# Channel attention with an ELU feed-forward on one core: six row groups multiplied as split float32r parts, squares summed in PSUM

## The chip, the cores and the metric

One core of a Trainium2 chip runs the whole program in one launch. The metric is device time in microseconds (us), from a few runs of the same kernel on the same chip; lower is better. Inputs are float32, except that the two weight matrices are read as 64-bit numbers and converted on the chip.

## The reference, cut to what matters

```python
# q, k, v: (4, 6080, 256); w_in: (256, 2048); w_out: (2048, 256)
qn = q / (np.linalg.norm(q, axis=1, keepdims=True) + 1e-06)
kn = k / (np.linalg.norm(k, axis=1, keepdims=True) + 1e-06)
s = kn.transpose(0, 2, 1) @ qn / tau          # (4, 256, 256)
a = np.exp(s - s.max(-1, keepdims=True))
a /= a.sum(-1, keepdims=True) + 1e-09
x = (v @ a).reshape(24320, 256)
h = x @ w_in
out = np.where(h > 0, h, np.exp(np.minimum(h, 0)) - 1) @ w_out
```

For each of the four batches a 256 x 256 matrix of products of k and q (the gram) is summed over 6080 rows, scaled by the norms of the columns of q and k, and put through a softmax. The result is multiplied into w_in once per batch, so that the long part is v times a 256 x 2048 matrix, ELU, and a product with w_out.

## The kernel before, in words

**Engines.** TensorE (PE) multiplies. ScalarE (ACT) and VectorE (DVE) apply ELU and split numbers into a float32r part and a residue; three passes of float32r parts (high by high, high by low, low by high) then stand for one float32 product. Float32 operands can also be given to TensorE as they are; each such multiplication stands in the trace as two matmul records. GpSimd (POOL) and SyncE (SP) mostly issue DMAs.

**The head: batch 0's gram and norms.** The 6080 rows of q and k are cut into 23 full groups (two rows for each of 128 partitions, q and k together 0.5 MB) and a last "ragged" one. `load0` issues the loads from SP. For each group, `square_rows` (L183) squares q and k on ACT (L189, 128 x 1024 numbers) and adds the squares on DVE into `acc` (L190); three tiles of squares take turns. `gram0_item` multiplies the group five steps later in the program (`BEHIND = 5`): four float32 multiplications of 128 x 128 by 128 x 256 (`multiply`, L496), that is eight records, which add into two banks of PSUM. PE, DVE and ACT run in the order in which the code is written (a manual schedule). When the squares are summed, `norms0` folds the two halves of `acc` on DVE (L221), sums over the partitions with four narrow matmuls into `pn` (L224), takes the root on ACT (L203), works out the reciprocals on DVE and writes a diagonal matrix `dg` (L236). `spread` (L262) turns that into a row for every partition with a matmul. Then come the softmax (`softmax0`, L269 to L283), the transposes of its result (L290) and the products of w_in with it (L323). Between these steps PE gets `early_items`: single rows of batch 1's gram, which add into the PSUM tile `pe`.

**PSUM.** There are eight banks of 128 x 512 float32 numbers. Two belong to the tag "gram", three to "w", three to "o". In the kernel before, the three banks of "o" are three tiles: `pe` (the gram of batch 1; later the ring `gram_ring`: grams, norms, transposes and the products with w_in of the later batches) and `po_1` for two halves `dt` of the output (`po_of["o"]`, later used by every second chunk). The sums of squares stand in SBUF (`new_acc`).

**The rest of the program.** Four chunks of batch 0 are run in an order written out by hand (`take`). All else, from about 235 us on, is a list of operations with costs and due times, which a planner puts in an order for each engine (`plan_half`, `plan_rows`, `plan_soft`, `plan_s`, `best_plan`). The change does not touch the planner, its costs or its due times. In this part PE writes `po` (L1387 to L1389) and `pe` (rows of the next batch's gram at L1524, products with w_in at L1425 to L1427), and ACT reads finished sums out of them: the output copies (L1118, `o_both<-po`), the scaled products (L1430, `w<-pe,sums`), the roots of the norms (L1593), the transposed softmax (L1657).

**How waits are set.** The program is written with tiles. The framework looks, tile by tile, for accesses that must not be reordered (a read after a write, a write after a read), and sets semaphore waits between the engines: a reader of a tile waits for the write it depends on, and a later writer of the tile waits for that reader.

Of the kernel before, what the change touches and what calls it, by code (L numbers as in the profile page):

```python
# [9 lines left out]
F32 = mybir.dt.float32  # L10
F32R = mybir.dt.float32r
# [45 lines left out]
def channel_attention_then_elu_ffn(ctx: ExitStack, tc, q, k, vT, tau, w_in, w_out, outT):  # L57
# [8 lines left out]
    nc = tc.nc  # L66
    B, N, C = q.shape
# [112 lines left out]
            fill_left(raw, b)  # L180
        return raw

    def square_rows(raw, acc, first, sq=None):  # L183
        if first:
            nc.scalar.activation(acc, raw, AF.Square)
            return
        if sq is None:
            sq = work.tile([P, 2, 2, C], F32, tag="sq", bufs=1, name="sq")
        x = nc.scalar.activation(sq, raw, AF.Square)  # L189
        return x.ins, nc.vector.tensor_add(acc, acc, sq).ins  # L190

    def new_acc(b):
        return work.tile([P, 2, 2, C], F32, tag="acc", bufs=1, name=f"acc_{b}")
# [291 lines left out]
    half = {c: scratch(c, k=DT) for c in range(M)}  # L485
    sq1 = scratch(M - 1, k=2 * 2).rearrange("p (t r) c -> p t r c", t=2)

    acc = new_acc(0)
    pg0 = [ps.tile([P, 2, C], F32, tag="gram", bufs=KT, name=f"gram_0_{ct}") for ct in range(KT)]
    wi64, wo64, vraw, vts = {}, {}, {}, {}  # L490
    state = {}

    def multiply(raw, r, gram, first, last):

        for ct in range(KT):
            nc.tensor.matmul(  # L496
                gram[ct], raw[:, 1, r, ct * P : ct * P + P], raw[:, 0, r, :], start=first[ct], stop=last[ct]
            )
# [4 lines left out]
    with tc.manual_schedule(engines={nc.sync.engine}):  # L503
# [38 lines left out]
            load0(x)  # L542
        raw1 = [scratch(x, k=2 * 2).rearrange("p (t r) c -> p t r c", t=2) for x in range(M)]

        def gram0_item(x):
            raw = raws.pop(x)
            for r in range(2):
                multiply(raw, r, gram0, [x + r == 0] * KT, [x == FULL - 1 and r == 1] * KT)
            if x + DEEP < FULL:
                load0(x + DEEP)  # L550
            if x + DEEP == FULL - 1:
                wi64[0] = load_w_in(0)

        for x in range(FULL):
            if x >= BEHIND:
                gram0_item(x - BEHIND)
            summed = square_rows(raws[x], acc, x == 0, squares[x % 3])
            if x == 16:
                square_rows(ragged, acc, False, squares[0])
                for r in range(2):  # L560
                    multiply(ragged, r, gram0, none, none)
                itau = tiny.tile([P, 1], F32, name="itau")
                nc.vector.reciprocal(itau, tau_sb)
# [6 lines left out]
        def go_on(part, n):  # L570
            for _ in range(n):
                next(part, None)

        for x in range(FULL - BEHIND, FULL):
            if x == FULL - 2:
                go_on(parts[0], 1)
                pn, dg, rk, nm = norms0(acc, lambda: go_on(parts[0], 2))
                go_on(parts[0], 2)
                go_on(parts[1], 1)
            gram0_item(x)  # L580

        pe = ps.tile([P, KT, C], F32, tag="o", bufs=8 - KT - WB, name="pe")
        gram1 = [pe[:, ct, :] for ct in range(KT)]

        def early_items(n, count=[0]):
            for _ in range(n):
                x, r = divmod(count[0], 2)
                count[0] += 1
                multiply(raw1[x], r, gram1, [x == 0 and r == 0, False], [False, (x, r) == (EARLY - 1, 1)])

        spread(pn, dg)
        vraw[1] = load_v(1)
        raw1.append(work.tile([P, 2, 2, C], F32, tag="raw", bufs=5, name="raw_early"))
# [15 lines left out]
        at_once(parts[1])  # L609
        for kt in range(KT):  # L610
            split_v_lo(0, vraw[0], vts[0], kt)
        early_items(3)
        aT0 = transpose_a(a0)
        go_on(first_w_out, 1)
        early_items(3)
# [137 lines left out]
    def s_part(fq, x, name):  # L753
# [3 lines left out]
    steps = [(c, f) for c, lo, hi in pieces for f in range(lo, hi)]  # L757
    es, gs, pos = {}, {}, {}
    po_of = {
        "o": [ps.tile([P, CH], F32, tag="o", bufs=8 - KT - WB, name=f"po_1{dt}") for dt in range(DT)],  # L760
        "gram": [ps.tile([P, CH], F32, tag="gram", bufs=KT, name=f"po_0{dt}") for dt in range(DT)],
    }

# [973 lines left out]
```

## Time and profile before

| | us |
|---|---|
| median of three runs | 2063.54 (2063.24 to 2063.66) |
| the profiled execution's own time | 2063.12 |
| its span | 2061.3 |
| PE busy in the span | 2054.8 |
| POOL busy in the span | 60.7 |

The profile is of one execution. A row of its timeline gives the start in us from the span's start, the length in us, the engine, the line of the kernel, the operation, output<-input, the shapes, and how often it stands there; in brackets, how long the engine was idle before it and what ended the idle time. Matmuls overlap: a record is longer than the distance to the next one, and its end is modelled. The granted TensorE clock is 1.0 throughout.

### The profile page before, as it was taken

Reading aid. Unit: us, or ns where it says so; the run is one execution under the profiler, and the core shown is the slowest. Engines: PE = TensorE matmul, PEld = TensorE weight load, DVE = VectorE, ACT = ScalarE, POOL = GpSimd, SP = SyncE. Lnnn points to the kernel's source line nnn. Section 1 sums busy time; section 2 is a strip of 40 time slices with the busy share of each in tenths; the row PEclk is TensorE's granted clock in tenths of the full one; section 3 lists DMA queues with packets and bytes.
Section 4 is the critical chain, followed back from the end, with each engine's and each line's share of the span. In section 5 each row is a group of like instructions: output and inputs, shape, how many; then the busy total and the mean of one; then the engine's idle time right before and its main releaser. Section 6 shows DMA issues by size and latency. Waiting matters only on the chain.

```text
span 2061.3 us, 28054 instructions
## 1 busy us (share of the span) xinstructions
PE 2054.8 (100%) x9976; PEld 1812.9 (88%) x9976; DVE 1669.3 (81%) x2597; ACT 1721.0 (83%) x3120; POOL 60.7 (3%) x118
## 2 busy tenths in 40 slices
PE   9999999999999999999999999999999999999999
PEld 8888888899888888888988888888888888888888
DVE  7988989888889787887887878788789777677775
ACT  6888789897888888888888888888887788887886
POOL 0000000000100000000000000000001000000000
PEclk9999999999999999999999999999999999999999
DMA  9453232212332121121322212212124110110000
GB/s 360 130 151 102 102 108 72 86 49 96 101 109 68 61 87 57 62 71 44 114 93 93 78 36 89 66 62 77 42 100 135 41 57 16 41 56 16 21 30 21
DMA packets 71805, 164.94 MB, mean 80 GB/s; under 512 B 7536, under 2 KB 16752, under 8 KB 69616
## 3 DMA queue, kind: packets, MB, share of 16 engines
q1 hardware_dynamic: 55968, 118.53, 16.9%
q0 software_dynamic: 15408, 44.11, 6.8%
q8 instruction: 78, 1.28, 0.3%
q14 instruction: 63, 0.52, 0.1%
q10 hardware_dynamic: 288, 0.51, 0.1%
HBM read 100.40 MB, written 31.20 MB: 64 GB/s over the span
## 4 chain that ended last, share of the span: by engine, by line
PE 99%; ACT 0%; DVE 0%; DMA 0%; SPq 0%; issue 0%; ACTq 0%
PE bank_b L1329 16%; PE po L1387 15%; PE po L1388 14%; PE po L1389 14%; PE bank_e L1329 11%; PE bank_a L1329 11%; PE pe L1524 4%; PE gram L496 2%; PE po L422 1%; PE po L420 1%; PE po L421 1%; PE ph L380 1%; PE ph L381 1%; PE ph L382 1%; PE pe L1427 1%; PE pe L1426 1%
## 5 line engine op out<-in xcount | busy, mean ns | idle before, releaser
L1387 PE MATMUL po<-g,wo 128*128 128x512 f32 (+1 forms) x938 | 354.1, 377 | 0.0
L1388 PE MATMUL po<-g,wo 128*128 128x512 f32 (+1 forms) x938 | 353.4, 377 | 0.0
L1389 PE MATMUL po<-g,wo 128*128 128x512 f32 (+1 forms) x938 | 353.4, 377 | 0.0
L1360 ACT ACTIVATE more_e<-more_e 128x512 f32<-128x512 f32 (+1 forms) x563 | 344.6, 633 | 2.4
L1369 DVE TENSOR_TENSOR g<-more_e,g 128x512 fp32r<-128x512 f32 (+1 forms) x374 | 252.6, 681 | 54.7 <-ACT g L1366 50.1
L1366 ACT CAST g<-more_e 128x512 fp32r<-128x512 f32 (+1 forms) x374 | 228.6, 620 | 42.7 <-DVE more_e L1363 27.1
L1389 PEld LDWEIGHTS po<-g,wo 128*128 128x128 f32 x938 | 177.4, 189 | 22.8
L1387 PEld LDWEIGHTS po<-g,wo 128*128 128x128 f32 x938 | 177.5, 189 | 21.9 <-ACT o_both L1118 0.2
L1363 DVE SCALAR_TENSOR_TENSOR more_e<-more_e,bank_b 128x512 f32<-128x512 f32 (+1 forms) x141 | 96.0, 681 | 124.3 <-ACT more_e L1360 124.0
L1388 PEld LDWEIGHTS po<-g,wo 128*128 128x128 f32 x938 | 177.6, 189 | 21.2
L1357 ACT ACTIVATE more_e<-bank_b 128x512 f32<-128x512 f32 (+1 forms) x141 | 83.8, 595 | 126.5 <-PE bank_b L1329 125.8
L1387 PE MATMUL po<-wp,wo 128*128 128x512 f32 (+1 forms) x470 | 177.4, 378 | 0.1
L1388 PE MATMUL po<-wp,wo 128*128 128x512 f32 (+1 forms) x470 | 177.1, 377 | 0.0
L1389 PE MATMUL po<-wp,wo 128*128 128x512 f32 (+1 forms) x470 | 177.1, 377 | 0.0
L1369 DVE TENSOR_TENSOR wp<-more_e,wp 128x512 fp32r<-128x512 f32 (+1 forms) x189 | 128.6, 681 | 33.1 <-ACT wp L1366 31.8
L1329 PE MATMUL bank_e<-term,wp 128*128 128x512 f32 (+1 forms) x528 | 141.4, 377 | 0.0
L1366 ACT CAST wp<-more_e 128x512 fp32r<-128x512 f32 (+1 forms) x189 | 116.9, 620 | 21.1 <-DVE more_e L1363 17.8
L1338 DVE TENSOR_TENSOR bank_e<-bank_b,e 128x512 f32<-128x512 f32 (+1 forms) x176 | 121.1, 688 | 7.5 <-ACT e L1336 4.9
L1342 DVE TENSOR_TENSOR e<-bank_b,e 128x512 f32<-128x512 f32 (+1 forms) x176 | 119.6, 680 | 4.9 <-PE bank_b L1329 4.5
L1329 PE MATMUL bank_a<-term,wp 128*128 128x512 f32 (+1 forms) x456 | 122.0, 376 | 0.0
L1524 PEld LDWEIGHTS pe<-rows 128*128 128x128 f32 x804 | 110.4, 191 | 6.7
L1524 PE MATMUL pe<-rows 128*128 128x256 f32 x804 | 111.2, 275 | 0.0
(323 smaller groups left out, 4718.2 us busy)
## 6 DMA issues: line engine op xcount, KB each, us to landing
v<-in_v_dram SPq DMA_DIRECT2D x13, 1024.0 KB, 5.0
out_dram<-o_both SPq DMA_DIRECT2D x48, 256.0 KB, 2.0
wi<-wi_scr POOLq DMA_DIRECT2D x12, 1024.0 KB, 5.5
w<-in_q_dram SPq DMA_DIRECT2D x34, 256.0 KB, 2.7
w<-in_k_dram SPq DMA_DIRECT2D x34, 256.0 KB, 2.9
v<-in_v_dram SPq DMA_DIRECT2D x8, 992.0 KB, 4.8
more<-in_q_dram SPq DMA_DIRECT2D x30, 256.0 KB, 2.6
more<-in_k_dram SPq DMA_DIRECT2D x30, 256.0 KB, 2.9
```

Of the source, the lines that this page charges most:

```text
L1329: nc.tensor.matmul(into, ws[x], y, start=(begin and k == 0), stop=(k == 2), skip_group_check=True)
L1338: up = op(DVE, 0.605 * share, t + DUE["up"], lambda: nc.vector.tensor_add(ve, vb, p7.slot[:, 0:n]), [m6, keep], uses=[bank_b, bank_e, p7])
L1342: last = op(DVE, 0.605 * share, t + DUE["last"], lambda: nc.vector.tensor_add(vp(), vb, vp()), [m5, up], uses=[bank_b, p7])
L1357: nc.scalar.activation(ev(), h(), AF.Relu, scale=-1.0)
L1360: nc.scalar.activation(ev(), ev(), AF.Exp, scale=-1.0)
L1363: nc.vector.scalar_tensor_tensor(ev(), ev(), -1.0, h(), op0=ALU.add, op1=ALU.max)
L1366: nc.scalar.copy(g_part(g, 0, n), halves(ev()))
L1369: nc.vector.tensor_sub(g_part(g, 1, n), halves(ev()), g_part(g, 0, n).bitcast(F32))
L1387: nc.tensor.matmul(o, wo[:, f, 0, ds], hi, start=begin, stop=False)
L1388: nc.tensor.matmul(o, wo[:, f, 1, ds], hi, start=False, stop=False)
L1389: nc.tensor.matmul(o, wo[:, f, 0, ds], lo, start=False, stop=end)
L1524: nc.tensor.matmul(pg, r.tile[:, kx, 1, z, cs], in_turns(r.tile[:, qx, 0, z, :]), start=(g == begun and ct == 0 and z == 0 and m == 0), st ...
```

## The change

Three things are changed.

1. Six of the 23 groups (7, 10, 13, 16, 18 and 20) are split into a float32r part and a residue. The residues are made by GpSimd (`tensor_sub`); the float32r parts by GpSimd for groups 7, 16, 18 and 20, and by ACT for 10 and 13. The parts lie in a tile of the tag "vt", of which there are two. Such a group is multiplied in twelve float32r passes (`multiply_split`) instead of four float32 multiplications.
2. The sums of batch 0's squares stand in PSUM: in the first two of the three banks of tag "o". The last addition writes its sum to a tile in SBUF.
3. The three banks of "o" are made one tile, `out_banks`, for the whole program; the two `po_1` and `pe` are now slices of it.

Besides, the norms are taken one group later (before group 22 instead of group 21), and one of the early items is moved from behind the spread to ahead of it.

```diff
@@ square_rows @@
-    def square_rows(raw, acc, first, sq=None):
+    def square_rows(raw, acc, first, sq=None, to=None):
...
-        return x.ins, nc.vector.tensor_add(acc, acc, sq).ins
+        return x.ins, nc.vector.tensor_add(acc if to is None else to, acc, sq).ins
@@
-    acc = new_acc(0)
+    out_banks = ps.tile([P, (8 - KT - WB) * CH], F32, tag="o", bufs=1, name="out_banks")
+    acc = out_banks[:, 0 : 2 * CH].rearrange("p (t r c) -> p t r c", t=2, r=2)
...
+    def split_rows(raw, own):
+        parts = work.tile([P, 2, 2, 2, C], F32R, tag="vt", bufs=2, name="parts")
+        (nc.gpsimd.tensor_copy if own else nc.scalar.copy)(parts[:, 0], raw)
+        nc.gpsimd.tensor_sub(parts[:, 1], raw, parts[:, 0].bitcast(F32))
+        return parts
+
+    def multiply_split(parts, r, gram, last):
+        for ct in range(KT):
+            for m, (kx, qx) in enumerate(((0, 0), (0, 1), (1, 0))):
+                nc.tensor.matmul(
+                    gram[ct], parts[:, kx, 1, r, ct * P : ct * P + P], parts[:, qx, 0, r, :], start=False, stop=last and m == 2
+                )
@@ the loop over the groups @@
+        SPLIT0 = {7: True, 10: False, 13: False, 16: True, 18: True, 20: True}
+        split0 = {}
...
-                multiply(raw, r, gram0, [x + r == 0] * KT, [x == FULL - 1 and r == 1] * KT)
+                if x in split0:
+                    multiply_split(split0[x], r, gram0, x == FULL - 1 and r == 1)
+                else:
+                    multiply(raw, r, gram0, [x + r == 0] * KT, [x == FULL - 1 and r == 1] * KT)
...
-            summed = square_rows(raws[x], acc, x == 0, squares[x % 3])
+            if x == FULL - 1:
+                squared = new_acc(0)
+            square_rows(raws[x], acc, x == 0, squares[x % 3], squared if x == FULL - 1 else None)
+            if x in SPLIT0:
+                split0[x] = split_rows(raws[x], SPLIT0[x])
...
-            if x == FULL - 2:
+            if x == FULL - 1:
                 go_on(parts[0], 1)
-                pn, dg, rk, nm = norms0(acc, lambda: go_on(parts[0], 2))
+                pn, dg, rk, nm = norms0(squared, lambda: go_on(parts[0], 2))
...
-        pe = ps.tile([P, KT, C], F32, tag="o", bufs=8 - KT - WB, name="pe")
+        pe = out_banks[:, 2 * CH : 3 * CH].rearrange("p (k c) -> p k c", k=KT)
...
+        early_items(1)
         spread(pn, dg)
...
-        early_items(3)
+        early_items(2)
         aT0 = transpose_a(a0)
@@
-        "o": [ps.tile([P, CH], F32, tag="o", bufs=8 - KT - WB, name=f"po_1{dt}") for dt in range(DT)],
+        "o": [out_banks[:, dt * CH : (dt + 1) * CH] for dt in range(DT)],
```

Three places show what this does to the built program. The first is ACT in the head, at groups 10 to 14 (`raw_10`, `raw_11`, `raw_12`, then two in `room`; `sq`, `scr` and `sq_107` are the three tiles of squares); after the change, lines behind the new functions have numbers 16 to 27 higher. Before:

```order
L189 ACTIVATE scr<-raw_10_140 128x1024
L189 ACTIVATE sq_107<-raw_11_143 128x1024
L189 ACTIVATE sq<-raw_12_146 128x1024
L189 ACTIVATE scr<-room_87 128x1024
L189 ACTIVATE sq_107<-room_87 128x1024
```

After:

```order
L189 ACTIVATE scr<-raw_10_140 128x1024
L497 CAST parts<-raw_10_140 128x1024
L189 ACTIVATE sq_107<-raw_11_143 128x1024
L189 ACTIVATE sq<-raw_12_146 128x1024
L189 ACTIVATE scr<-room_87 128x1024
L497 CAST parts<-room_87 128x1024
L189 ACTIVATE sq_107<-room_87 128x1024
```

ACT has a float32r copy behind the square of group 10 and another behind that of group 13; GpSimd's residues follow these copies.

The second place is PE at the end of the head (`raw_21` and `raw_22` are the last two groups, `pn` the norms, `dg` the diagonal matrix, `pe` or `out_banks` the early items of batch 1). Before:

```order
L224 MATMUL pn<-ones,acc_91 128x1 x4
L496 MATMUL gram_0_92<-raw_21_230 128x256
L496 MATMUL gram_1_93<-raw_21_230 128x256
L496 MATMUL gram_0_92<-raw_21_230 128x256
L496 MATMUL gram_1_93<-raw_21_230 128x256
L496 MATMUL gram_0_92<-raw_22_239 128x256
L496 MATMUL gram_1_93<-raw_22_239 128x256
L496 MATMUL gram_0_92<-raw_22_239 128x256
L496 MATMUL gram_1_93<-raw_22_239 128x256
L262 MATMUL pn<-dg,ones 128x256
L496 MATMUL pe<-scr 128x256 x6
L290 MATMUL pt<-ident,a_385 128x128 x4
```

After:

```order
L512 MATMUL gram_1_93<-raw_21_244 128x256
L224 MATMUL pn<-ones,acc_354 128x1 x4
L512 MATMUL gram_0_92<-raw_22_256 128x256
L512 MATMUL gram_1_93<-raw_22_256 128x256
L512 MATMUL gram_0_92<-raw_22_256 128x256
L512 MATMUL gram_1_93<-raw_22_256 128x256
L512 MATMUL out_banks<-scr 128x256 x2
L262 MATMUL pn<-dg,ones 128x256
L512 MATMUL out_banks<-scr 128x256 x4
L290 MATMUL pt<-ident,a_453 128x128 x4
```

The norm sums stand behind group 21 instead of ahead of it, and two of the six early multiplications ahead of the spread.

The third place is PE far behind the head, in the planned part at about 325 us, where the order of the instructions stays and their waits change (in brackets: the engine whose semaphore the instruction waits for). `po_465` is the second half of an output that ACT copies out, `pe` takes rows of batch 1's gram. Before:

```order
L1387 MATMUL po_465<-g_2027,wo 128x512
L1388 MATMUL po_465<-g_2027,wo 128x512
L1389 MATMUL po_465<-g_2027,wo 128x512
L1524 MATMUL pe<-rows 128x256 x6
L1524 MATMUL pe<-rows 128x256 [waits Activation_49]
L1524 MATMUL pe<-rows 128x256 [waits DVE_49]
```

After:

```order
L1414 MATMUL out_banks<-g_2091,wo 128x512 [waits Activation_49]
L1415 MATMUL out_banks<-g_2091,wo 128x512
L1416 MATMUL out_banks<-g_2091,wo 128x512
L1551 MATMUL out_banks<-rows 128x256 x6
L1551 MATMUL out_banks<-rows 128x256 [waits Activation_49]
L1551 MATMUL out_banks<-rows 128x256 [waits DVE_49]
```

The first of these now waits for ACT's copy of the other half of the output (of `po_464`), which stands just ahead of it in the program. The seventh row product waited for ACT before as well, for the rounding of its rows long before; now it waits for ACT's copy of `po_465`, and that copy itself waits for the sixth row product.

## Prediction

> **What bounds the kernel now.** I read the page first (busy time, then the chain that ended last), then the timeline of the head, then that of the planned part.
>
> ```profile
> span 2061.3 us, 28054 instructions
> PE 2054.8 (100%) x9976; PEld 1812.9 (88%) x9976; DVE 1669.3 (81%) x2597; ACT 1721.0 (83%) x3120; POOL 60.7 (3%) x118
> PE 99%; ACT 0%; DVE 0%; DMA 0%; SPq 0%; issue 0%; ACTq 0%
> ```
>
> PE is the chain for 99% of the span. So a pass saved on PE is worth its length, and a wait of PE costs its length, wherever it stands; the other engines count only where PE waits for them. The head:
>
> ```profile
> 7.21 12.32 PE L496 MATMUL gram<-room 128*128 128x256 f32 x56 [0.16 <-DMA room<-in_k_dram]
> 15.33 1.06 ACT L189 ACTIVATE scr<-room 128x1024 f32<-128x1024 f32 x1 [0.21 <-DMA room<-in_k_dram]
> 19.37 7.07 PE L496 MATMUL gram<-raw 128*128 128x256 f32 x32
> 21.37 1.06 ACT L189 ACTIVATE scr<-raw 128x1024 f32<-128x1024 f32 x1 [0.96 <-DMA raw<-in_k_dram]
> 29.73 13.98 PE L496 MATMUL gram<-room 128*128 128x256 f32 x64
> 40.67 1.23 DVE L190 TENSOR_TENSOR acc<-acc,scr 128x1024 f32<-128x1024 f32 x1
> 41.93 0.69 DVE L221 TENSOR_TENSOR acc<-acc 128x512 f32<-128x512 f32 x1
> 43.55 0.95 PE L224 MATMUL pn<-ones,acc 128*128 128x1 f32 x8
> 44.36 3.70 PE L496 MATMUL gram<-raw 128*128 128x256 f32 x16
> 44.53 0.17 ACT L203 ACTIVATE y<-pn 128x4 f32<-128x4 f32 x1 [2.38 <-PE pn L224]
> 46.57 0.29 DVE L236 TENSOR_SCALAR dg<-ident,ry 128x128 f32<-128x128 f32 x1 [0.18 <-issue]
> 47.89 0.59 PE L262 MATMUL pn<-dg,ones 128*128 128x256 f32 x2
> 48.32 2.75 PE L496 MATMUL pe<-scr 128*128 128x256 f32 x12
> 51.16 0.31 PEld L290 LDWEIGHTS pt<-ident,a 128*128 128x128 f32 x3 [0.32 <-ACT a L279]
> ```
>
> From 7.21 on PE runs group after group: seven by 19.37, eight from 29.73 to 43.55, so 1.73 each. The group at 19.37 is group 8; hence group 7 begins at 17.64 and group 10 at 22.83. The data of groups 7 and 10 have landed only at 15.3 and 21.4, when ACT, which waited for them, starts their squares. That leaves 2.3 and 1.5 between landing and multiplication; at group 20 (square at 35.9, multiplied at 41.8) there are six.
>
> **The change, part by part.**
>
> *Fewer passes.* Twelve float32r passes of this shape stand in the planned part:
>
> ```profile
> 326.02 1.50 PE L1524 MATMUL pe<-rows 128*128 128x256 f32 x12
> 327.36 0.38 PE L1329 MATMUL bank_e<-term,scr_r 128*128 128x512 f32 x1
> ```
>
> They take 1.34, from 326.02 to 327.36, instead of 1.73: 0.39 a group, 2.3 for six. This is all that the change removes from PE.
>
> *The parts of groups 7 and 10.* No row shows GpSimd copying or subtracting; the nearest are these, and ACT's cast of the same size:
>
> ```profile
> 0.77 0.20 POOL masks.py:197 MEMSET ident<- 128x128 f32 x1
> 0.91 0.53 POOL L506 MEMSET ragged<- 128x512 f32 x1
> 1.48 0.28 POOL masks.py:199 TENSOR_SCALAR_AFFINE_SELECT ident<-ident 128x128 f32<-128x128 f32 x1
> 417.25 1.05 ACT L1493 CAST rows<-w 128x1024 fp32r<-128x1024 f32 x1
> ```
>
> 384 more numbers cost the memset 0.33, so 1024 take about 0.97; at the pace of the select, which also reads, 1.57 ((0.28 - 0.10) / 128 a number, with 0.10 fixed). I take 1.3 for a copy. A residue reads two operands: at best DVE's 1.23 for the same shape, at worst two select passes, 3.1; I take 2.2, the middle. Group 7: copy from 15.4 to 16.7, residue to 19.0; PE is there at 17.6 and waits 1.4. Group 10: square to 22.4, ACT's cast to 23.5, residue to 25.8; PE, two groups after its first wait, is there at 23.9 and waits 1.9. Even with a residue at 1.23 group 10 is not ready before 24.8, 2.0 after PE got there in the trace. Groups 13, 16, 18 and 20 come out ready by the same count (30.7 against 32.3; 34.3 against 37.1; 37.9 against 40.2; 42.1 against 43.3). Behind group 20 PE stands 3.3 - 2.3 = 1.0 late.
>
> The Trainium skill (GPSIMD Engine Reference, section 3.1) gives a GpSimd addition of 2048 numbers 4497 ns; half of that is an estimate of 2.25 for a residue, and no run here shows it. With it the head's sum moves by under 0.1.
>
> *Squares in PSUM, and ACT's two copies.* An addition on DVE that reads and writes PSUM costs what one in SBUF costs:
>
> ```profile
> L1338 DVE TENSOR_TENSOR bank_e<-bank_b,e 128x512 f32<-128x512 f32 (+1 forms) x176 | 121.1, 688 | 7.5 <-ACT e L1336 4.9
> L1369 DVE TENSOR_TENSOR g<-more_e,g 128x512 fp32r<-128x512 f32 (+1 forms) x374 | 252.6, 681 | 54.7 <-ACT g L1366 50.1
> ```
>
> 7 ns on 512 numbers is 0.3 over the 23 additions. ACT's cast for group 13 pushes the next square by some 0.8. The fold then ends at about 43.6 instead of 42.6. PE, at group 21's end, is at 46.3: no wait.
>
> *The norms one group later.* `pn` runs from 46.3 to 47.1 (0.8 to the next group in the trace). From its end to the second `dg` it takes 2.4 (44.5 to 46.9), so the spread can start at 49.6; group 22 and one early item (0.86: twelve records in 2.6 are three items) bring PE to 49.7. The spread starts 1.8 later than at 47.89, with one early item done more. From the spread to the transposes that wait for ACT it is 3.4 (47.7 to 51.1); two early items instead of three fill 0.86 less of that, and PE waits that much longer. So the transposes stand at 53.1 instead of 51.2: **the head loses 1.9**. Its bounds: with prompt parts it would gain 1.4 (2.3 less 0.86); with copies at 1.57 and residues at 3.1 group 20 is late as well, and it loses 4.7.
>
> *The three banks as one tile.* In the built program every ACT or DVE read of `out_banks` waits for all its earlier writes, whichever bank they touch, and every later write waits for the read. In the head that costs nothing: the readers are done long before. In the planned part PE writes `po` and `pe` in close turns while ACT reads the other bank. One place in full:
>
> ```profile
> 325.25 0.59 ACT L1118 COPY o_both<-po 128x512 f32<-128x512 f32 x1
> 325.38 0.38 PE L1387 MATMUL po<-g,wo 128*128 128x512 f32 x1
> 326.77 0.60 ACT L1118 COPY o_both<-po 128x512 f32<-128x512 f32 x1
> 1603.71 0.56 ACT L1118 COPY o_both<-po 128x496 f32<-128x496 f32 x1
> 1603.84 0.38 PE L1389 MATMUL po<-g,wo 128*128 128x512 f32 x1
> 1604.33 0.48 PE L1387 MATMUL po<-wp,wo 128*128 128x512 f32 x1
> 1604.65 0.38 PE L1388 MATMUL po<-wp,wo 128*128 128x512 f32 x1
> ```
>
> The last four rows show what such a wait is when it is a true one: PE's write at 1604.33 starts 0.06 after the copy that it needs (1603.71 + 0.56), and its next pass follows after 0.32 instead of 0.21, so 0.1 is lost on top. At 325.38 PE now has to wait for the copy of the other half, to 325.25 + 0.59 + 0.06 = 325.9: 0.5 to 0.6. The copy at 326.77 now waits for the sixth of the twelve row products (326.58 + 0.28 for its record, + 0.03 as from 44.50 to ACT's 44.53: 326.89), ends at 327.49, and the seventh (326.69) waits for it until 327.55: 0.86.
>
> I did the same for every write of PE whose new wait ends after PE's time in the trace, carrying each delay on to all engines. The readers:
>
> ```profile
> L1118 ACT COPY o_both<-po x70: 553/592/641, 325.3 to 1988.7; 128x512 f32<-128x512 f32 x48, 128x496 f32<-128x496 f32 x22
> L1430 ACT ACTIVATE w<-pe,sums x22: 667/688/730, 538.4 to 1587.7; 128x512 f32<-128x512 f32 x22
> ```
>
> There are 23 such writes: 13 behind output copies (0.22 to 0.86, together 8.2), six behind the scaled products of L1430 (three of 0.89, three under 0.3: 3.1), two behind the roots of the norms at 498.6 and 1500.8 (1.9), two behind the transposed softmax at about 1520 (0.6). Together 13.8, and 0.1 for each restart 2.3: **16.1**. Bounds: the fourteen longest alone, with no restart, are 11.8; 23 of the full 0.86 are 19.8.
>
> **Sum.** 2063.12, the profiled execution's own time (1.8 over its span), + 1.9 + 16.1 = 2081.1. The median lies 0.4 above that execution, so **2081.5**, slower by 0.9%. Less than 0.2%, 4.1 us, I count as no change: a measurement of this kernel tells little below that.
>
> **The rivals.**
>
> *Not slower: the tile's new waits do not bind.* If PE reaches its writes late enough, or the waits are met earlier than the records say, only the head is left: 2063.5 + 1.9 = 2065.4, and 2062.1 with prompt parts; neither is told from no change. For it: PE's records end by a model. Against: PE's wait at 1604.33 shows that the records and the semaphores agree to 0.06. It decides at 325.38: does PE wait for the copy there or not. 0.07.
>
> *The waits bind, but half is given back*, since a PE that is late finds other operands ready. In the trace PE's span has only 6.5 without a record, most of it before 7.21, so there is little to give back. 16.1 / 2 + 1.9 gives 2073.5. 0.13.
>
> *Plain column order is dear.* Every float32r pass of the planned part reads its columns in turns from two halves; the new ones read them in plain order. If a pass then took as long as a record of a plain float32 multiplication (1.73 / 8 = 0.216), a group would take 2.6 instead of 1.34: six times 1.25 more, less about 1.2 as PE then comes later to group 10: 6.3, 2087.8. For it: no row shows a float32r pass in plain order. Against: a float32 record does more than one pass's work at that length. 0.1.
>
> *GpSimd at the upper price, or held up by DVE*: the head loses 4.7 instead of 1.9, 2084.3. A mechanism would be that the two engines shut each other out where both read SBUF: the fold (L221, 0.69) and the conversions behind it read two operands from SBUF while group 20's residue may still run (to 42.1 in my count, to 46 at the upper price). 0.12.
>
> The Trainium skill (SBUF — State Buffer, Who interferes with whom) says that a DVE instruction with two SBUF inputs and a GpSimd instruction that reads SBUF block each other, and one with a single SBUF input does not. By that rule the additions into PSUM leave GpSimd free, and the fold would be the one to be held; no run here shows it yet.
>
> **How the numbers follow.** The forecast 0.58, the rivals 0.07, 0.13, 0.1, 0.12. The range runs from 2074 (11.8 for the waits and a head that gains a little) to 2088 (the upper head or the dear passes with the full waits); it leaves out the first rival and about half of the second. Of the first rival's 0.07 I give 0.05 to no change and 0.02 to faster by over 0.2%, which would need the whole saving and more. The rest, 0.93, is slower.
>
> **What would show it.** In the new profile: waits of PE for ACT's `o_both<-out_banks`, for `w<-out_banks` and for the roots, some 23 with 0.5 to 0.9 each, first at about 327; waits of 1 to 2 for GpSimd at groups 7 and 10 and none at 13 to 20; a float32r group in 1.34; the transposes at about 53; POOL's busy time up by some 18 (four copies, six residues). The prediction is wrong if PE's records run through at 327, or if PE's waits lie in the head alone.

## The result, and the profile after

The changed kernel takes 2086.08 us (median of five runs, 2084.56 to 2086.9) against 2063.66 for the kernel before (five runs, 2063.24 to 2064.28): a ratio of 1.0106, 95% interval 1.0095 to 1.0118, slower by 1.1%. The profiled execution takes 2084.56, 21.4 more than the profiled one of before. These are its span, busy times and chain:

```profile
span 2082.8 us, 28118 instructions
PE 2059.8 (99%) x10000; PEld 1809.7 (87%) x10000; DVE 1670.2 (80%) x2597; ACT 1726.1 (83%) x3122; POOL 79.0 (4%) x128
PE 95%; ACT 2%; DMA 1%; DVE 1%; issue 0%; POOL 0%; SPq 0%; DVEq 0%; ACTq 0%
```

PE is the chain for 95% instead of 99%; ACT, DVE and the DMA now have a part in it. PE's busy time grew by only 5.0 of the 21.4; most of the rest is waiting. For whom PE waits, the view of waits tells (engine, line, who is waited for; us in total, times, the longest):

```profile
PE out_banks L1414 <- ACT o_both L1145: 4.6, 8, 0.7
PE out_banks L1414 <- ACT w L1457: 2.6, 4, 0.8
PE gram L505 <- POOL parts L498: 2.4, 2, 1.8
PE out_banks L1414 <- ACT y L1620: 1.7, 2, 1.2
PE pt L290 <- ACT a L279: 1.5, 2, 1.0
PE gram L512 <- DMA room<-in_k_dram: 1.3, 1, 1.3
PE bank_e L1356 <- DVE more_e L1390: 1.3, 1, 1.3
```

Three of the rows are `out_banks`, the shared tile. `pt` and `gram L505` are the head. The DMA wait was 0.2 before and `bank_e <- more_e` 0.7.

To see where the time enters I set every matmul of after beside the same one of before, by its place in PE's order, and took the difference of the two starts. It is 3.1 at the head's end (from about 59 us on) and stays 3.1 until the planned part. Behind the head it grows by 18.3, of which 15.7 in 28 jumps of 0.13 to 1.39. The head, in the timeline of after:

```profile
7.45 10.60 PE L512 MATMUL gram<-room 128*128 128x256 f32 x48 [1.29 <-DMA room<-in_k_dram]
15.19 1.04 POOL L497 CAST parts<-room 128x1024 fp32r<-128x1024 f32 x1 [13.43 <-DMA room<-in_k_dram]
16.31 2.36 POOL L498 TENSOR_TENSOR parts<-room,parts 128x1024 fp32r<-128x1024 f32 x1
18.73 1.58 PE L505 MATMUL gram<-parts 128*128 128x256 f32 x11 [0.56 <-POOL parts L498]
20.15 3.62 PE L512 MATMUL gram<-raw 128*128 128x256 f32 x16
25.72 1.57 PE L505 MATMUL gram<-parts 128*128 128x256 f32 x11 [1.83 <-POOL parts L498]
27.13 1.89 PE L512 MATMUL gram<-raw 128*128 128x256 f32 x8
32.12 1.78 PE L505 MATMUL gram<-parts 128*128 128x256 f32 x12
33.74 3.62 PE L512 MATMUL gram<-room 128*128 128x256 f32 x16
43.09 0.69 DVE L221 TENSOR_TENSOR acc<-acc 128x512 f32<-128x512 f32 x1
44.95 1.89 PE L512 MATMUL gram<-raw 128*128 128x256 f32 x8
46.68 0.95 PE L224 MATMUL pn<-ones,acc 128*128 128x1 f32 x8
47.66 0.17 ACT L203 ACTIVATE y<-pn 128x4 f32<-128x4 f32 x1 [4.96 <-PE pn L224]
50.16 0.59 PE L262 MATMUL pn<-dg,ones 128*128 128x256 f32 x2
54.27 0.31 PEld L290 LDWEIGHTS pt<-ident,a 128*128 128x128 f32 x3 [0.64 <-ACT a L279]
```

Read as group starts, before and after: the long first row begins 0.24 later, behind a load (in a kernel without splits, below, by 1.2, so it is not the splits); group 8 begins at 20.15 instead of 19.37, group 11 at 27.13 instead of 24.56 (19.37 plus three groups of 1.73), group 21 at 44.95 instead of 43.55. So PE loses 0.5 at group 7, 1.8 at group 10, wins 1.2 over groups 13 to 20, and stands 1.4 late at group 21. The transposes wait until 54.27 instead of 51.16: 3.1.

The place in the planned part that the prediction worked out, in the timeline of after (the matching rows of before start at 325.38 and 326.02):

```profile
328.98 0.59 ACT L1145 COPY o_both<-out_banks 128x512 f32<-128x512 f32 x1
329.62 0.48 PE L1414 MATMUL out_banks<-g,wo 128*128 128x512 f32 x1 [0.36 <-ACT o_both L1145]
330.37 0.83 PE L1551 MATMUL out_banks<-rows 128*128 128x256 f32 x6
331.24 0.59 ACT L1145 COPY o_both<-out_banks 128x512 f32<-128x512 f32 x1 [0.63 <-PE out_banks L1551]
331.88 0.94 PE L1551 MATMUL out_banks<-rows 128*128 128x256 f32 x6 [0.68 <-ACT o_both L1145]
```

PE's write at 329.62 starts 0.05 behind the end of a copy that reads the other half; the next copy waits for the sixth of twelve row products that go to a third bank; the seventh, at 331.88, waits for that copy. The twelve products stood in one row of 1.50 before. No number passes between these banks; the waits come from their being one tile.

### The profile page after: what moved, and what is told of

Read it like the earlier page. It is cut to its first block, busy times and chain, and to the rows that moved or that the text cites. A ratio compares the mean times of both kernels' runs of the same rounds, so it can differ in the third digit from the quotient of the medians.

```text
span 2082.8 us, 28118 instructions
## 1 busy us (share of the span) xinstructions
PE 2059.8 (99%) x10000; PEld 1809.7 (87%) x10000; DVE 1670.2 (80%) x2597; ACT 1726.1 (83%) x3122; POOL 79.0 (4%) x128
## 4 chain that ended last, share of the span: by engine, by line
PE 95%; ACT 2%; DMA 1%; DVE 1%; issue 0%; POOL 0%; SPq 0%; DVEq 0%; ACTq 0%
PE bank_b L1356 16%; PE bank_e L1356 11%; PE bank_a L1356 10%; PE out_banks L1414 7%; PE out_banks L1416 7%; PE out_banks L1415 7%; PE po L1414 7%; PE po L1415 7%; PE po L1416 7%; PE out_banks L1551 4%; PE ph L381 1%; PE ph L380 1%; PE ph L382 1%; PE out_banks L422 1%; PE gram L512 1%; PE po L420 1%
## 5 line engine op out<-in xcount | busy, mean ns | idle before, releaser
L1414 PE MATMUL out_banks<-g,wo 128*128 128x512 f32 (+1 forms) x500 | 190.3, 381 | 7.6 <-ACT o_both L1145 4.0
L1416 PE MATMUL out_banks<-g,wo 128*128 128x512 f32 (+1 forms) x500 | 188.4, 377 | 0.0
L1415 PE MATMUL out_banks<-g,wo 128*128 128x512 f32 (+1 forms) x500 | 188.4, 377 | 0.0
L1414 PE MATMUL po<-g,wo 128*128 128x512 f32 (+1 forms) x438 | 165.2, 377 | 0.0
L1415 PE MATMUL po<-g,wo 128*128 128x512 f32 (+1 forms) x438 | 164.8, 376 | 0.0
L1416 PE MATMUL po<-g,wo 128*128 128x512 f32 (+1 forms) x438 | 164.8, 376 | 0.0
L1551 PEld LDWEIGHTS out_banks<-rows 128*128 128x128 f32 x804 | 110.2, 191 | 8.1 <-ACT o_both L1145 1.3
L1414 PEld LDWEIGHTS out_banks<-g,wo 128*128 128x128 f32 x500 | 94.5, 189 | 24.2 <-ACT o_both L1145 7.1
L1551 PE MATMUL out_banks<-rows 128*128 128x256 f32 x804 | 111.6, 275 | 0.7 <-ACT o_both L1145 0.7
L1356 PEld LDWEIGHTS bank_e<-term,wp 128*128 128x128 f32 x528 | 99.8, 189 | 12.9
L1390 DVE SCALAR_TENSOR_TENSOR more_e<-more_e,bank_a 128x512 f32<-128x512 f32 (+1 forms) x139 | 94.1, 677 | 17.0 <-ACT more_e L1387 16.0
```

Of the source, the lines that this page charges most:

```text
L1356: nc.tensor.matmul(into, ws[x], y, start=(begin and k == 0), stop=(k == 2), skip_group_check=True)
L1390: nc.vector.scalar_tensor_tensor(ev(), ev(), -1.0, h(), op0=ALU.add, op1=ALU.max)
L1414: nc.tensor.matmul(o, wo[:, f, 0, ds], hi, start=begin, stop=False)
L1415: nc.tensor.matmul(o, wo[:, f, 1, ds], hi, start=False, stop=False)
L1416: nc.tensor.matmul(o, wo[:, f, 0, ds], lo, start=False, stop=end)
L1551: nc.tensor.matmul(pg, r.tile[:, kx, 1, z, cs], in_turns(r.tile[:, qx, 0, z, :]), start=(g == begun and ct == 0 and z == 0 and m == 0), st ...
```

## The experiments

Each kernel below was timed against the kernel before on its chip; "the delay" is the difference of matmul starts described above, in the profiled execution. The first loads alone move it by up to 1.2 from one execution to the next, so small differences of it between two kernels say little. The line numbers in their rows differ by a few.

**The shared tile alone.** The kernel before, with `pe` and the two `po_1` cut from one tile:

```diff
+    out_banks = ps.tile([P, (8 - KT - WB) * CH], F32, tag="o", bufs=1, name="out_banks")
-        pe = ps.tile([P, KT, C], F32, tag="o", bufs=8 - KT - WB, name="pe")
+        pe = out_banks[:, 2 * CH : 3 * CH].rearrange("p (k c) -> p k c", k=KT)
-        "o": [ps.tile([P, CH], F32, tag="o", bufs=8 - KT - WB, name=f"po_1{dt}") for dt in range(DT)],
+        "o": [out_banks[:, dt * CH : (dt + 1) * CH] for dt in range(DT)],
```

> The kernel before, with nothing changed but that pe and the two po_1 are slices of one tile of three banks; the squares are summed in SBUF and no group is split. Theory (the shared tile's waits cost the planned part): the head ends as before, the planned part loses what it lost in the changed kernel behind the head, 21.4 - 3.1 = 18.3, so 2081 to 2083, with some 23 waits of PE behind ACT's reads of out_banks. Rival (the loss behind the head comes from the split groups or the late head, and the waits are met in time): 2063 to 2065.

2082.0 (2081.51 to 2082.81), ratio 1.0087 (1.0072 to 1.0102): slower by 18, with no split and no sum in PSUM. PE's waits:

```profile
PE out_banks L1388 <- ACT o_both L1119: 4.6, 8, 0.7
PE out_banks L1388 <- ACT w L1431: 2.6, 4, 0.8
PE gram L497 <- DMA room<-in_k_dram: 2.3, 1, 2.3
PE out_banks L1388 <- ACT y L1594: 1.7, 2, 1.2
```

The three `out_banks` rows are those of after to the tenth. The delay at the end is 19.5; 1.2 of it is in the head, behind a late load (2.3 here), so 18.3 lie behind the head, as in after.

**Everything but the shared tile.** The changed kernel with its sums in a PSUM pool of their own, which is closed before the three output banks are made as three tiles:

```diff
-    out_banks = ps.tile([P, (8 - KT - WB) * CH], F32, tag="o", bufs=1, name="out_banks")
-    acc = out_banks[:, 0 : 2 * CH].rearrange("p (t r c) -> p t r c", t=2, r=2)
+    acc_life = ExitStack()
+    acc_ps = acc_life.enter_context(tc.tile_pool(name="acc_ps", bufs=1, space=bass.MemoryType.PSUM))
+    acc = acc_ps.tile([P, 2 * CH], F32, name="acc_banks").rearrange("p (t r c) -> p t r c", t=2, r=2)
...
+        acc_life.close()
+        ps_o = ctx.enter_context(tc.tile_pool(name="ps_o", bufs=8 - KT - WB, space=bass.MemoryType.PSUM))
```

> The changed kernel with the sums of squares in a PSUM pool of their own that is closed before pe is made; pe and the two po_1 are three tiles again, as in the kernel before. Splits, squares in PSUM and norms stay as in the changed kernel. Theory: only the head's 3.1 is left, 2066 to 2067.5, and PE has no wait for ACT's reads of po or pe. Rival (the delay of the planned part comes with the head): 2080 or more.

2068.02 (2066.92 to 2070.33), ratio 1.0021 (1.0011 to 1.0030). The delay is 3.5 at the head's end and 4.05 at the end: the tail's 18 are gone, the head's loss is all there. The median is 0.5 above what was expected; a later run shows two losses that come in some executions and not in others (below), and either may be the reason. What is left in PE's waits, beside the transposes' 1.5 for the softmax:

```profile
PE gram L506 <- POOL parts L499: 2.9, 2, 1.6
```

**Half a dose.** The kernel before, with only the two `po_1` in one tile:

```diff
+    pair_banks = ps.tile([P, DT * CH], F32, tag="o2", bufs=1, name="pair_banks")
-        "o": [ps.tile([P, CH], F32, tag="o", bufs=8 - KT - WB, name=f"po_1{dt}") for dt in range(DT)],
+        "o": [pair_banks[:, dt * CH : (dt + 1) * CH] for dt in range(DT)],
```

> The kernel before, with only the two output banks po_1 as halves of one tile, pe a tile of its own; no splits, sums in SBUF. Theory (a tile shared by several products is taken and given back as a whole, so each product's first write waits for the readers of the other bank; counting the waits by their places in the trace): +6.0 us for the pair alone, up to 7 with the later waits for VectorE: 2069.5 to 2071. Rival (the cost lies in having the tile next to another purpose, pe's bank, and two banks of one purpose already overlap): 2063 to 2065.

2070.46 (2069.55 to 2071.62), ratio 1.0031 (1.0019 to 1.0043): 6.6 more; the delay grows by 7.0 behind the head. The counting of waits holds at the second dose too, and the same write waits (at 325.38 before):

```profile
326.66 0.48 PE L1388 MATMUL pair_banks<-g,wo 128*128 128x512 f32 x1 [0.36 <-ACT o_both L1119]
```

**The sums back in SBUF.** The changed kernel with `acc = new_acc(0)` and three output tiles, so without the shared tile too:

```diff
-    acc = out_banks[:, 0 : 2 * CH].rearrange("p (t r c) -> p t r c", t=2, r=2)
+    acc = new_acc(0)
```

> The changed kernel with the sums of squares in SBUF and three tiles, so that DVE's additions read two operands from SBUF while GpSimd reads rows. Theory 1 (both engines share a read port and shut each other out for a whole instruction, as the Trainium skill says in SBUF - State Buffer, Who interferes with whom): ten GpSimd passes of 1.04 to 2.38 and the additions of 1.23 take turns from 15 us on; residues and additions stretch, the fold ends several us after 43.8, and the time is 2070 to 2080. Theory 2 (they do not disturb each other): like the kernel with the sums in a PSUM pool of their own, 2066 to 2067.5.

2077.72 (2076.9 to 2078.89), ratio 1.0067 (1.0052 to 1.0082). GpSimd's residue and cast and DVE's additions of squares in the head, by groups of lines (mean ns of one behind the comma), here:

```profile
L497 POOL TENSOR_TENSOR parts<-room,parts 128x1024 fp32r<-128x1024 f32 x5 | 15.5, 3107 | 1.0 <-ACT parts L496 0.7
L496 POOL CAST parts<-room 128x1024 fp32r<-128x1024 f32 x4 | 7.5, 1883 | 14.0 <-DMA room<-in_k_dram 13.9 <-PE gram L504 0.2
L190 DVE TENSOR_TENSOR acc<-acc,sq 128x1024 f32<-128x1024 f32 x15 | 29.6, 1972 | 1.8 <-ACT sq L189 0.4
```

And in after, with the sums in PSUM:

```profile
L498 POOL TENSOR_TENSOR parts<-room,parts 128x1024 fp32r<-128x1024 f32 x5 | 11.9, 2381 | 3.5 <-DMA room<-in_q_dram 3.2
L497 POOL CAST parts<-room 128x1024 fp32r<-128x1024 f32 x4 | 4.1, 1037 | 14.1 <-DMA room<-in_k_dram 13.4 <-PE gram L505 0.7
L190 DVE TENSOR_TENSOR out_banks<-out_banks,sq 128x1024 f32<-128x1024 f32 x15 | 18.5, 1233 | 3.9 <-ACT sq L189 2.7
```

With both of DVE's operands in SBUF the two engines hold each other up: 2.38 becomes 3.11, 1.04 becomes 1.88, 1.23 becomes 1.97. The sums are then ready late, and PE waits for the fold at `pn`:

```profile
54.33 1.87 PE L224 MATMUL pn<-ones,acc 128*128 128x1 f32 x8 [5.16 <-DVE acc L221]
```

And the table by stretches of time (busy time of PE, PEld, DVE, ACT and POOL with instruction counts, the granted clock, DMA share, GB/s) shows behind it:

```profile
56.00:60.00 4.00, 4.00 (x10) 3.23 (x11) 3.02 (x12) 3.25 (x6) 0.00 (x0) 0.50 0.92 297
```

So the sums in PSUM do earn something: the delay at the head's end is 13.4 here and 3.5 with them in PSUM. Not all of the 9.9 between them is DVE's lateness itself. Behind the wait of 5.16 the granted clock is at half, and from `pn` to the second group of transposes it takes 10.2 (54.33 to 64.56) instead of the 7.6 of after (46.68 to 54.27): 2.6 go to the clock.

**Columns in turns.** The kernel with the banks apart, its split passes reading q's columns in turns from two halves, as the passes of the planned part do (the columns of the six groups then add into other columns of the gram):

```diff
-  gram[ct], parts[:, kx, 1, r, ct * P : ct * P + P], parts[:, qx, 0, r, :], start=False, stop=last and m == 2
+  gram[ct], parts[:, kx, 1, r, ct * P : ct * P + P], in_turns(parts[:, qx, 0, r, :]), start=False, stop=last and m == 2
```

> As the kernel with the sums in a PSUM pool of their own, but the twelve passes of a split group read the columns of q in turns from two halves, as all other float32r passes of the program do; the columns of these six groups are then added in another order than those of the other groups, so the output is not the reference's. Theory (plain column order makes a pass 0.135 instead of 0.112): a split group takes 1.34 instead of 1.62, six times 0.28 = 1.7 less, as far as PE doesn't wait for parts or norms: 2064.5 to 2066. Rival (a group in the head costs 1.62 for another reason, for example going from float32 to float32r and back): no difference to plain order, 1.62 a group.

2068.22 (2066.43 to 2070.16), ratio 1.0022 (1.0012 to 1.0031): no gain over the plain order. Group 13 and the start of the next:

```profile
33.05 1.69 PE L506 MATMUL gram<-parts 128*128 128x256 f32 x12
34.58 3.62 PE L513 MATMUL gram<-room 128*128 128x256 f32 x16
```

The distance is 1.53 here and 1.62 in after (32.12 to 33.74). That is a real but small difference: the starts of single passes lie 0.112 apart in turns and 0.120 in plain order, 12 x 0.008 = 0.1 a group. The rest of 1.62 is in the records: a plain float32 group that stands ahead of a split one shows 1.54 to the next start, and 1.73 elsewhere, so a split group costs 1.62 - 0.19 = 1.43, not 1.62. I had read 1.62 as the price and expected a gain of 1.7; of the 0.6 that six groups would give, nothing is left in the time, with waits here of 1.42 for the first load and 2.06 at group 10. So the theory had the direction right and the size wrong, and the rival, no difference at all, is refuted by the spacing of the passes and not by the time.

**The norms where they were.** The kernel with the banks apart, the norms ahead of group 21 again:

```diff
-            if x == FULL - 1:
+            if x == FULL - 2:
```

> The kernel with the banks apart, with the norms taken ahead of group 21 again instead of behind it. Theory (the softmax's a starts a fixed 3.4 us after the root, so the place of pn sets the head's delay): pn comes earlier by one f32 group, 1.73 us, as soon as the sums' fold is ready; the fold ends at 43.8, group 20 at about 43.1, so pn begins at 43.8 at the earliest. The head's delay falls from 3.5 to between 1.5 and 2.3, the time from 2068.0 to 2066 to 2067. Rival (the spread to the transposes sets it, the norms' place hardly matters): the delay stays above 3 and the time at 2068, since group 21 then only runs behind pn instead of ahead of it.

2069.06 (2066.22 to 2070.73), ratio 1.0021 (1.0012 to 1.0031): by the median, no gain; neither theory's number. The ten runs lie in two heaps, four from 2066.22 to 2067.15, six from 2068.94 to 2070.73. The profiled execution is of the upper heap. Its timeline and its table by stretches show one loss:

```profile
26.29 2.34 PE L506 MATMUL gram<-parts 128*128 128x256 f32 x11 [1.95 <-POOL parts L499]
28.43 2.76 PE L513 MATMUL gram<-raw 128*128 128x256 f32 x8
31.02 1.89 PE L513 MATMUL gram<-ragged 128*128 128x256 f32 x8
```

```profile
26.00:28.00 2.00, 1.71 (x9) 1.71 (x10) 1.58 (x3) 1.42 (x2) 0.24 (x1) 0.69 1.05 406
28.00:30.00 2.00, 2.00 (x7) 1.73 (x7) 1.34 (x2) 2.00 (x3) 1.36 (x1) 0.50 1.05 403
30.00:32.00 2.00, 2.00 (x10) 1.70 (x10) 1.90 (x2) 1.42 (x2) 1.99 (x2) 0.95 1.06 398
```

Behind PE's wait of 1.95 for GpSimd the granted clock falls to half for 3.4 us (in the three stretches 1.72 us of full clock are missing). Eleven passes take 2.14 to the next start instead of 1.41 (25.72 to 27.13 in after), the float32 group behind them 2.59 instead of 1.73: 1.6 lost. Without that the head's delay of 4.2 would be 2.6, 0.9 less than the 3.5 of the kernel with late norms; the lower heap's 2066.2 to 2067.2 is what the theory had forecast. The same execution shows a second loss: at about 577 us the delay grows by 1.8, where DVE waited 1.80 for a transfer into `term` and PE 1.06 for DVE; no part of the change is near, and why the transfer was late I did not follow. The heaps lie 3.0 apart by their means, about as far as the two losses together. How the two are spread over the other nine executions one profile can't tell, so the cause of the heaps stays open.

**Only the late groups.** The kernel with the banks apart, groups 7 and 10 plain:

```diff
-        SPLIT0 = {7: True, 10: False, 13: False, 16: True, 18: True, 20: True}
+        SPLIT0 = {13: False, 16: True, 18: True, 20: True}
```

> The kernel with the banks apart, with only the last four groups (13, 16, 18 and 20) split; 7 and 10 stay plain f32. Theory (TensorE's two waits for GpSimd's parts, 0.56 and 1.83 us, cost more than the two groups save, 2 x 0.3): the head gains 2.4 - 0.6 = 1.8 where nothing else binds, the delay at the head's end falls from 3.5 to about 1.7, time 2066 to 2067. Rival (the waits hide in a later one, on the square sums' fold or on a load): the delay falls by less than 0.5, time 2067.5 to 2068.5.

2066.13 (2065.47 to 2067.68), ratio 1.0011 (1.0002 to 1.0020); the delay at the head's end falls from 3.5 to 2.0. So groups 7 and 10 cost more than they save, as the theory had it (forecast 1.7). PE's only wait for GpSimd is now one of 0.8, at group 13.

**A longer wait.** To test the clock, the kernel with the banks apart writes the residue of group 10 twice (`times` is 2 there and 1 elsewhere):

```diff
+        for _ in range(times):
             nc.gpsimd.tensor_sub(parts[:, 1], raw, parts[:, 0].bitcast(F32))
```

> The kernel with the banks apart, with GpSimd's residue of group 10 written twice, so that TensorE's wait ahead of that group's second pass grows from 1.6-1.95 to about 4.0 us (one more residue, 2.37). Theory of the clock (a gap of about 2 us on TensorE lets the granted clock fall to half for some 2.5 us behind it, which costs 1.5 to 2; at 1.6 to 1.95 it happens in about half of the executions): with a gap of 4 it happens in every one; the profile shows a granted clock of 0.5 behind group 10, and every run lies near 2067.3 + 2.4 + 1.7 = 2071.4, in one cluster. Rival (the fall has another cause, and the gap only happens to stand before it): the profile shows a clock of 1.0 there, or the runs still lie in two clusters 2 us apart, about 2069.7 and 2072.

2073.34 (2070.67 to 2075.31, five runs), ratio 1.0044 (1.0029 to 1.0058). The wait is 4.49, and the clock falls behind it again, as the rival had denied:

```profile
28.94 2.02 PE L507 MATMUL gram<-parts 128*128 128x256 f32 x11 [4.49 <-POOL parts L500]
```

```profile
28.00:30.00 2.00, 1.06 (x8) 1.06 (x9) 1.65 (x2) 2.00 (x3) 1.45 (x2) 0.96 1.06 408
30.00:32.00 2.00, 2.00 (x8) 1.77 (x8) 1.54 (x2) 2.00 (x3) 2.00 (x2) 0.50 0.99 377
```

Its fastest run is as slow as the slowest of the kernel without the second residue (2070.33). The profiled execution lost 1.9 at 581 us to a late transfer, as above; without that it would be at 2071.4, as forecast. But the five runs don't lie in one heap there as the theory had asked, and only one of them is profiled. That the clock falls every time at such a gap is not shown.

**Late groups and early norms.** The kernel with the banks apart, groups 13 to 20 split and the norms ahead of group 21:

```diff
-        SPLIT0 = {7: True, 10: False, 13: False, 16: True, 18: True, 20: True}
+        SPLIT0 = {13: False, 16: True, 18: True, 20: True}
-            if x == FULL - 1:
+            if x == FULL - 2:
```

> The kernel with the banks apart, only groups 13, 16, 18 and 20 split, and the norms ahead of group 21 again; the conversion steps stay between root and softmax. Theory: without the gaps of 2 us no run loses to the clock, and pn starts at 43.8 to 44.0 (the fold's end) instead of 45.55; the softmax's a starts 3.4 behind the root, at 48.4 instead of 49.96, so the head's delay falls from 2.0 to about 0.6 to 1.2: 2064.5 to 2065.3. Rival (the spread, which in the program order stands behind group 22, sets the softmax): no gain over 2066.1.

2064.94 (2063.97 to 2066.84), ratio 1.0007 (0.9998 to 1.0016): 1.2 less than with late norms (0.9, if each is set against the kernel before on its own chip), and inside the forecast range. The mechanism is not shown as clearly: the profiled execution waited 1.4 for a load and 2.06 at group 13, and its delay is 2.35 instead of the forecast 0.6 to 1.2. It shows a gap of 2.06 with no fall of the clock (1.00 from 30 to 40 us):

```profile
32.61 1.57 PE L506 MATMUL gram<-parts 128*128 128x256 f32 x11 [2.06 <-POOL parts L499]
```

So a gap of two us does not always do it; the gap of 2.06 in the kernel with columns in turns was not followed by a fall either (granted clock 1.0).

**The best that these parts give.** As the last, with both parts of group 13 by GpSimd and two conversion steps of DVE (L140, L143) moved from ahead of the softmax to behind it:

```diff
-        SPLIT0 = {7: True, 10: False, 13: False, 16: True, 18: True, 20: True}
+        SPLIT0 = {13: True, 16: True, 18: True, 20: True}
-            if x == FULL - 1:
+            if x == FULL - 2:
-                go_on(parts[0], 2)
-            go_on(parts[0], 1)
+            go_on(parts[0], 3)
```

> The kernel with the banks apart, groups 13, 16, 18 and 20 split with both parts by GpSimd, norms ahead of group 21, and the two conversion steps of part 0 (L140 and L143, on VectorE between the root and the softmax's a) moved behind the softmax. Theory: no wait for parts, the root at or before the place it has in the kernel before, and a starts 0.9 us sooner after it: head delay between -1 and +0.8, time 2062.5 to 2064.5. Rival (the conversion is needed sooner, so the products behind the softmax wait for it instead): 2065 to 2067.

2064.61 (2063.77 to 2066.82), ratio 1.0004 (0.9994 to 1.0013): not told from the kernel before, just above the theory's range and below the rival's. The profiled execution is the slowest of the ten, and 2.0 of its delay of 3.8 is the late transfer again. Moving the conversion only moved the wait: the softmax now waits on DVE for the spread, and PE's products with w_in wait for a bank that DVE empties (L340) after the conversions that stand ahead of it.

```profile
49.96 0.42 DVE L277 TENSOR_TENSOR a<-a,pn 128x256 f32<-128x256 f32 x1 [0.81 <-PE pn L262]
58.70 1.13 PE L323 MATMUL pw<-wf,aT 128*128 128x256 f32 x4 [0.41 <-DVE wp L340]
```

No version that I ran beats the kernel before.

## Why the prediction was right, and where its sizes were off

The forecast was slower, 2081.5 in 2074 to 2088; it is 2086.08. Both terms of the sum have the sign that the prediction gave them, and both were too small: the head lost 3.1 instead of 1.9, the shared tile 18.3 instead of 16.1. The tile's cause is the one forecast; in the head one step was wrong. The median lies 1.5 above the profiled execution instead of 0.4. That all this still falls inside the range is in part the range's width: its upper end stood for dear passes or a slow GpSimd, and neither came.

*The shared tile: shown.* The tile alone costs 18.3 behind the head, everything else without it nothing there but 0.5, two of its three banks 7.0. Of the 28 jumps, 23 stand at writes to the shared tile, and they sum to 13.7; the prediction had 23 writes and 13.8. The two worked examples, 0.5 to 0.6 and 0.86, came as 0.52 and 0.84. What was missed is an indirect part: five jumps, together 2.0, at the banks of the products that DVE and ACT feed (`bank_e`, `bank_b`). Three of them (0.6, where PE's wait for `more_e` grew from 0.7 to 1.3, and twice 0.45) come at the same places in both kernels that share a tile without splits; with the banks apart one of 0.28 at another place is all. That fits ACT and DVE being held at the tile themselves and reaching those banks later, but the way of each delay through the engines I did not follow, so it is argued, not shown. Of the rest, 2.4 stand within eight matmuls behind the jumps, 0.1 for most of them: the price of a restart, where the prediction had 2.3 for 23.

*The rival "half is given back": did not happen.* Only nine steps of 0.06 to 0.15 are given back, 0.8 together; otherwise the delay grows. The prediction weighed this rival by a wrong reading: of the 6.5 without a PE record only 1.2 lie before 7.21, and 4.5 in the last 11 us. Its conclusion stands, as there is still next to nothing between.

*Fewer passes: the term that was mis-sized.* "They take 1.34 ... 0.39 a group, 2.3 for six." In plain column order a pass takes 0.120 instead of the 0.112 of the passes that the row was taken from, and a group 1.43: 0.30 saved, 1.8 for six. The rival of dear plain order had the right direction and a price more than ten times too high (it is 0.1, not 1.25, a group).

*GpSimd's waits.* The copy took 1.04 (forecast 1.3, bounds 0.97 to 1.57), the residue 2.36 to 2.39 (2.2, bounds 1.23 to 3.1). PE lost, restarts and all, 0.8 at group 7 and 2.1 at group 10 (forecast 1.4 and 1.9: the sums at the group starts above, with the 0.3 saved put back), and did not wait at the four later groups, as counted. Half of the addition of 2048 numbers in the Trainium skill (GPSIMD Engine Reference, section 3.1), an estimate, would have been 2.25 for the residue; the trace is 5 to 6% above that. The fold ended at 43.8 (43.6 forecast) and made nobody wait.

*DVE and GpSimd shutting each other out: not in this kernel, but real.* The Trainium skill (SBUF — State Buffer, Who interferes with whom) says that a DVE instruction with at most one SBUF input does not contend with GpSimd, and that one with two contends with a GpSimd instruction that reads SBUF. The runs agree with both. GpSimd's times above are the first half. The second half is in the run with early norms, where the last residue ran from 42.14 to 44.53 and the fold, 0.69 long elsewhere, from 42.85 to 45.07:

```profile
42.14 2.39 POOL L499 TENSOR_TENSOR parts<-room,parts 128x1024 fp32r<-128x1024 f32 x1
42.85 2.22 DVE L221 TENSOR_TENSOR acc<-acc 128x512 f32<-128x512 f32 x1
```

The fold ended 0.54 behind the residue, so it did most of its own 0.69 after the residue's end. In after the residue was done at 42.36, ahead of the fold.

*The norms one group later: the step that failed.* "From the spread to the transposes that wait for ACT it is 3.4." The transposes need two things: the spread, and DVE's chain from the root through reciprocals, conversion and softmax. From the root to the second group of transposes it is 6.6 in before (44.53 to 51.16), in after (47.66 to 54.27) and in the runs with late norms. From the spread it is 3.3 in before and 4.1 in after (50.16 to 54.27), and where the spread does bind, in the three runs with early norms, 3.05 (and 7.3 from the root). So already in before it was the root's chain that the transposes waited for, and the spread had 0.2 to spare; with the norms one group later it has 1.05. The prediction took an interval between two steps of which the first does not set the second. So the right sum goes by the root. Counted from `pn`'s start it is 7.6 in before (43.55 to 51.16) and in after (46.68 to 54.27): with the prediction's own 46.3 for `pn` a loss of 2.7, and with a PE that is 0.4 later (0.24 of it the load, the rest the passes and waits above) the 3.1 of the trace.

*The median.* The profiled execution of after, 2084.56, is the fastest of its five; the other four are 2084.71 and 2086.08 to 2086.9. A fall of the clock behind group 10 (a wait of 1.83 here), worth 1.6, would account for the three, and so would the late transfer at about 577 us, worth 1.8 to 2.0 in three other kernels. After's own profile has neither: its clock is 1.0 throughout, and its delay does not grow there. So which of the two it is, if either, stays open.

## What to carry to other kernels

Banks or buffers that different engines use in close turns must not be slices of one tile where the framework orders accesses tile by tile: each use then waits for the others, and the price can be counted beforehand from the old trace, write by write, but add what the held engines hand on. A step that waits for several things has to be followed from each of them: the interval from the one that was last before says nothing once another is last. And an engine's own passes are to be priced from rows of the same access pattern.

## What the runs showed of the hardware

- Gaps on PE of 1.95 and 4.49 us were each followed by 3.4 us at half the granted clock (0.50 in the table by stretches), which cost 1.6. Behind gaps of 2.73 and 5.16 in the run with the sums in SBUF it was at half too. It stayed at 1.0 behind gaps of 1.83 (after), 2.06 (two kernels) and 2.27 (the load of the tile alone). The Trainium skill (TensorE: Matmul & The Clock Gate, Part 1) explains such falls by a window of 3.4 us that runs freely, so that what a gap does depends on where it falls. That one gap of about two us does it and a longer one doesn't agrees with that, and so does the length of the fall. The page has the clock fall after a whole window without work; the gap of 1.95 was shorter than a window, and there the measurement decides.
- A float32r pass of 128 x 128 by 128 x 256 costs 0.120 with its columns in plain order and 0.112 with the columns taken in turns from two halves.
- GpSimd casts 128 x 1024 float32 numbers to float32r in 1.04, and subtracts in 2.38. DVE adds into PSUM in place, 128 x 1024, in 1.233; in SBUF it takes 1.225.
